# A transformer block in one kernel: the first layer norm's roots, the order of its loads and the order of the PSUM pools in the prologue

## The chip, the cores and the metric

The kernel runs on one core of one Trainium2 chip. The metric is the device time of one execution in microseconds (us); the time given for a kernel is the median of its runs.

The core has five engines, each with a queue of its own that is worked in order: TensorE (PE in the profile; its loads of stationary operands are shown apart, as PEld), VectorE (DVE), ScalarE (ACT), GpSimd (POOL) and SyncE (SP), which here issues nearly all transfers. Engines meet at semaphores. SBUF and PSUM are the two on-chip memories; matmuls write PSUM.

## The reference, cut to what matters

```python
S, D, H = 2048, 512, 32                      # batch 1, head size 16
def layernorm(x):                            # over the last axis, eps 1e-5
    return (x - mean(x)) / sqrt(var(x) + eps)

def attention(x, wqkv, wo):
    q, k, v = heads(x @ wqkv)
    p = softmax(einsum("bhqd,bhkd->bhqk", q, k) * Dh ** -0.5)
    return merge(einsum("bhqk,bhkd->bhqd", p, v)) @ wo

def gmlp(x, w_in, w_sp, b_sp, w_out):        # F = 1376, half of it 688
    z = gelu(x @ w_in)
    z1, z2 = z[..., :688], layernorm(z[..., 688:])
    return (z1 * (einsum("ts,bsf->btf", w_sp, z2) + b_sp)) @ w_out

h  = x + attention(layernorm(x), wqkv, wo)
h2 = h + gmlp(layernorm(h), w_in, w_sp, b_sp, w_out)
```

All arrays are float32, x is 2048 x 512.

## The kernel before

The 2048 rows are cut into 16 blocks of 128 rows (`sb`). Four stages follow each other: a prologue (layer norm of x and its projections), attention with the row maxima of the scores found ahead of their use, a stage per block of rows (h, the second layer norm, z), and the spatial product with the output. The first two stages are written inside `tc.manual_schedule` for TensorE, ScalarE, VectorE and SyncE: on these engines instructions stand in the order in which the program issues them; on GpSimd the framework orders them. Every change below lies in the prologue, but for the root `rstd_of`, which the second layer norm and that of z use too.

A product with more than half precision is made of three matmuls: operands are split into a high part (rounded, written by ScalarE or GpSimd) and a low part (the difference, by VectorE or GpSimd) in `split` (L77, L79 and L82 in the profile), and `mm3` (L85 to L87) multiplies high by high, high by low and low by high.

What happens to a block of x in the prologue:

- `load_x(sb)` (L261) asks for its 128 x 512 rows, 256 KB. All 10 buffers of tag `row` are shared with the pieces of the weights; `load_wv(d)` (L265) asks for a 128 x 512 piece of w_v and returns a function that splits it: the high part on ScalarE (for piece 1 on GpSimd), the low part on GpSimd.
- `stats` (L287, L288) finds mean and variance on VectorE; `scales` calls `rstd_of` for 1/sqrt(var + eps) and makes `nb` = -mean/sqrt (L301, L303).
- `rstd_of` (L92 to L109) takes a first guess from the bits of the number and improves it by three Newton steps. For one block (n = 1) a step is two instructions, each with operands that are one column; for more it is three.
- `normal` (L310) scales the block on ScalarE, in place.
- `turn_x` (L321) transposes it on TensorE into a PSUM tile `tp`; ScalarE copies the high part of the result into `xT[0]` and VectorE the low part into `xT[1]`.
- `proj_v` (L372 for blocks 0 and 1, else `mm3`) and `proj_qk` multiply; their accumulators come from `next_acc`, in turn two from pool `ps[0]` and one from `ps[1]`; `take` empties them (ScalarE and VectorE, L77 and L82, or VectorE alone, L382) and stores the result to DRAM.

Blocks 0 and 1 go through it one at a time, blocks 2 and 3 as a pair, blocks 4 to 15 in groups of four. `between` in `scales` lets the transposes of block 1 and the split of their result stand between the first and the second Newton step of blocks 2 and 3. While nothing is there to multiply, TensorE multiplies a tile of zeros, 16 times (L396).

In the later projections, the maxima of the first rows of scores are found between the products (`ahead`, `max_pair`, L203, L208). When the prologue's pools close, attention opens `ps_v` (one bank, the weighted sums `pv`, L628; the first time it is only written with a placeholder, L686) and `ps_s` (two tiles of two banks, the scores `s`, L617). They are allotted the banks that the prologue's pools had: pools are stacked in the order in which they are opened, and a tile waits for what its banks held before. Before the change that order is `pre_pt` (two banks), `pre_ps0` (two), `pre_ps1` (one). Each pair of key blocks in attention then goes: scores (L617), two maxima, `pv` of the pair before (L628), further maxima and scores, `pv`; ScalarE makes exponentials of the scores (L620).

Of the kernel before, what the change touches and what calls it, by code (L numbers as in the profile page):

```python
# [8 lines left out]
F32 = mybir.dt.float32  # L9
# [4 lines left out]
ALU = mybir.AluOpType  # L14
# [4 lines left out]
P = 128  # L19
S = 2048  # L20
D = 512
# [3 lines left out]
EPS = 1e-5  # L25
# [19 lines left out]
def block_kernel(ctx: ExitStack, tc: tile.TileContext, x, wqkv, wo, w_in, w_sp4, b_sp, w_out, out):  # L45
# [43 lines left out]
    def rstd_of(pool, var, n, between=lambda: None):  # L89

        hv = pool.tile([P, n], F32, name=f"rs_v{n}")
        nc.vector.tensor_scalar(hv, var, EPS, 0.5, op0=ALU.add, op1=ALU.mult)  # L92
        r = pool.tile([P, n], F32, name=f"rs_r{n}")
        nc.vector.tensor_scalar(r.bitcast(I32), hv.bitcast(I32), -0.5, GUESS,
                                op0=ALU.mult, op1=ALU.add)
        t = pool.tile([P, n], F32, name=f"rs_t{n}")
        for i in range(3):
            if i == 1:
                between()

            if n == 1:
                nc.vector.tensor_scalar(t, r, r, hv, op0=ALU.mult, op1=ALU.mult)
                u = pool.tile([P, 1], F32, name="rs_u", bufs=6)
                nc.vector.tensor_scalar(u, t, 1.5, r, op0=ALU.subtract, op1=ALU.mult)
                r = u
            else:
                nc.vector.tensor_mul(t, r, r)
                nc.vector.tensor_mul(t, t, hv)
                nc.vector.scalar_tensor_tensor(r, t, 1.5, r, op0=ALU.subtract, op1=ALU.mult)  # L109
        return r  # L110
# [135 lines left out]
    with ExitStack() as pre:  # L246
        p2 = pre.enter_context(tc.tile_pool(name="pre_2", bufs=2))
        pc = pre.enter_context(tc.tile_pool(name="pre_c", bufs=1))
        pt = pre.enter_context(tc.tile_pool(name="pre_pt", bufs=2, space=PSUM))
        ps = [pre.enter_context(tc.tile_pool(name=f"pre_ps{i}", bufs=2 - i, space=PSUM))  # L250
              for i in range(2)]
# [6 lines left out]

        def load_x(sb):
            xs[sb] = p2.tile([P, D], F32, name="xg", tag="row", bufs=10)  # L260
            nc.sync.dma_start(xs[sb], x[sb * P:(sb + 1) * P, :])  # L261

        def load_wv(d, eh="act"):
            t = p2.tile([P, 512], F32, name="wg", tag="row", bufs=10)
            nc.sync.dma_start(t, w4[:, d, 2 * D:])  # L265
            return lambda: split(wv[0][:, d, :], wv[1][:, d, :], t, eh, "pool")
# [16 lines left out]
        def stats(mv, *blocks):  # L283

            for sb in blocks:
                st = p2.tile([P, 6], F32, name="st")
                nc.vector.bn_stats(st, xs[sb])  # L287
# [6 lines left out]
        def scales(mv, between=lambda: None):  # L294
# [3 lines left out]
            rs = rstd_of(p2, t[:, :, 1], n, between)  # L298
            nb = p2.tile([P, n], F32, name=f"nb{n}")
            if n == 1:  # L300
                nc.vector.tensor_scalar(nb, rs, t[:, 0, 0:1], -1.0, op0=ALU.mult, op1=ALU.mult)  # L301
            else:
                nc.vector.scalar_tensor_tensor(nb, t[:, :, 0], -1.0, rs, op0=ALU.mult, op1=ALU.mult)  # L303
# [91 lines left out]
        for _ in range(16):  # L395
# [14 lines left out]
        with tc.manual_schedule(engines={E.PE, E.Activation, E.DVE, E.SP}):  # L410
# [14 lines left out]
            put = [load_wv(0), load_wv(1, "pool")]  # L425
            load_x(2)
            put.append(load_wv(2))
            load_x(3)
            put.append(load_wv(3))
            load_x(4)  # L430
            load_x(5)
            mv = [moments(1), moments(1), moments(2)]
            stats(mv[0], 0)
            normal = scales(mv[0])
            put[0]()
            put[1]()
            normal(0)
            stats(mv[1], 1)
            normal = scales(mv[1])
            put[2]()  # L440
            turn_x(0)
            load_x(6)
            put[3]()
            normal(1)
            stats(mv[2], 2, 3)
            chain = lambda d: d == 2 and normals.append(scales(mv[2], lambda: turn_x(1)))
            normals = []
            takes.append(proj_v(0, chain))
            normal = normals[0]
# [753 lines left out]
```

## Time and profile before

| what | us |
|---|---|
| median of 3 runs | 1889.48 |
| lowest and highest | 1888.72 and 1889.94 |
| the profiled execution | 1893.73 |
| its span, first to last instruction | 1891.8 |
| TensorE busy in the span | 1877.6 (99%) |
| VectorE, ScalarE, GpSimd busy | 1538.8, 1330.8, 209.3 |
| first steady matmul of the prologue (L85) | at 17.75 |
| first score of attention (L617) | at 173.28 |

A row of the timeline has the start, the length, engine and line, the operation, the tile written and those read, shapes and how many instructions are shown as one; in square brackets how long its engine had been idle and what ended that. Rows of a group have how many instructions, their busy time together and the mean of one in ns. Rows of a window have, for each engine, busy time and instructions, and at the end the granted clock of TensorE as a share, the share of the DMA engines and GB/s.

### The profile page before, as it was taken

The page shows a single profiled execution, that of the slowest core. Times are in us where ns is not written, and L with a number is a line of the kernel's source. Part 1 is how long each engine was busy: PE and PEld are TensorE (multiplying, and loading weights), DVE is VectorE, ACT ScalarE, POOL GpSimd, SP SyncE. Part 2 cuts the span into 40 slices and gives each one's busy share as a digit, 9 for nine tenths or more (in the row PEclk, how much of TensorE's full clock was granted, in tenths as well). Part 3 has the DMA queues.
Part 4 walks back from the last instruction along what each step waited for, and adds up shares of the span by engine and source line. Part 5 has one row for each costly group of instructions (what it writes and reads, how often), then busy time and mean ns, then how long its engine had stood idle before and what let it go on. Part 6 is the DMA issues. An engine that isn't in the chain of part 4 may idle for free.

```text
span 1891.8 us, 32405 instructions
## 1 busy us (share of the span) xinstructions
PE 1877.6 (99%) x11608; PEld 1065.0 (56%) x11608; DVE 1538.8 (81%) x3099; ACT 1330.8 (70%) x1733; POOL 209.3 (11%) x287
## 2 busy tenths in 40 slices
PE   9999999999999999999999999999999999999999
PEld 6865444444444444444444444444439999998887
DVE  6487999999999999999999999999926677867554
ACT  3334888888888888888888888888884444334221
POOL 2130000011010100000000000000010754001211
PEclk9999999999999999999999999999999999999999
DMA  6677111221120111021012011100024555677552
GB/s 188 186 192 192 43 24 27 49 53 28 38 56 22 47 38 25 19 51 32 14 44 36 23 30 38 24 16 14 10 78 138 163 167 170 215 216 238 177 185 75
DMA packets 148105, 159.82 MB, mean 84 GB/s; under 512 B 62952, under 2 KB 92664, under 8 KB 146408
## 3 DMA queue, kind: packets, MB, share of 16 engines
q1 hardware_dynamic: 143304, 146.48, 28.9%
q10 hardware_dynamic: 4608, 11.27, 1.6%
q8 instruction: 91, 1.49, 0.4%
q14 instruction: 70, 0.57, 0.1%
q0 software_dynamic: 32, 0.01, 0.0%
HBM read 101.16 MB, written 55.61 MB: 83 GB/s over the span
## 4 chain that ended last, share of the span: by engine, by line
PE 95%; DMA 2%; DVE 2%; issue 0%; POOL 0%; ACT 0%; SPq 0%; ACTq 0%; DVEq 0%; POOLq 0%
PE pv L628 27%; PE m L203 26%; PE s L617 13%; PE acc L85 6%; PE acc L87 6%; PE acc L86 6%; PE g L85 3%; PE g L86 3%; PE g L87 3%; DMA a<-in_w_sp 1%; PE tp L1093 0%; DMA g_scr<-q 0%; DMA h<-h_scr 0%; PE tp L804 0%; DMA rc<-r_scr 0%
## 5 line engine op out<-in xcount | busy, mean ns | idle before, releaser
L620 ACT ACTIVATE pt<-s 128x1024 f32<-128x1024 f32 x1024 | 993.2, 1030 | 147.4 <-PE s L617 145.0
L208 DVE TENSOR_REDUCE mx<-m 128x1 f32<-128x512 f32 x1511 | 959.0, 684 | 107.3 <-PE m L203 64.3
L203 PE MATMUL m<-kst,qst 48*128 48x512 f32 x1511 | 607.9, 448 | 0.0
L628 PE MATMUL pv<-pt,vst 128*32 128x512 f32 x4096 | 550.2, 605 | 0.7 <-ACT o L635 0.7
L617 PE MATMUL s<-qst,kst 50*128 50x512 f32 x2048 | 466.2, 428 | 2.0 <-DVE part L82 1.5
L203 PEld LDWEIGHTS m<-kst,qst 48*128 48x128 f32 x1511 | 263.8, 184 | 315.0 <-DVE mx L208 221.7
L617 PEld LDWEIGHTS s<-qst,kst 50*128 50x128 f32 x2048 | 223.6, 185 | 56.4 <-ACT pt L620 30.2
L203 PE MATMUL m<-uvs,qst 48*128 48x512 f32 x503 | 249.1, 496 | 0.0
L203 PEld LDWEIGHTS m<-uvs,qst 48*128 48x128 f32 x503 | 91.9, 183 | 208.1 <-DVE mx L208 205.3
L217 DVE CUSTOM_DVE_ANT_0 ab<-m,ab 128x512 f32<-128x512 f32 x252 | 171.8, 682 | 3.8 <-ACT ab L213 2.0
L628 PEld LDWEIGHTS pv<-pt,vst 128*32 128x32 f32 x4096 | 82.9, 108 | 161.0 <-issue 155.7
L213 ACT ACTIVATE ab<-m 128x512 f32<-128x512 f32 x251 | 151.0, 602 | 17.3 <-PE m L203 16.9
L79 POOL CAST mparts<-nm 128x16 fp32r<-128x16 f32 x32 | 6.3, 198 | 911.4 <-DVE nm L223 911.4
L747 ACT ACTIVATE ws<-a 128x512 fp32r<-128x512 f32 x80 | 45.8, 623 | 58.2 <-issue 37.4
L85 PE MATMUL acc<-wi,hT 128*128 128x344 f32 x256 | 83.1, 325 | 0.0
L87 PE MATMUL acc<-wi,hT 128*128 128x344 f32 x256 | 81.8, 319 | 0.0
L86 PE MATMUL acc<-wi,hT 128*128 128x344 f32 x256 | 81.7, 319 | 0.0
L819 ACT ACTIVATE z<-acc 128x344 f32<-128x344 f32 x64 | 29.2, 457 | 62.3 <-PE acc L87 54.8
L748 DVE TENSOR_TENSOR ws<-a,ws 128x512 fp32r<-128x512 f32 x80 | 56.5, 749 | 13.2 <-ACT ws L747 13.1
L85 PE MATMUL g<-b,ws 128*128 128x344 f32 x192 | 64.2, 334 | 0.0
L85 PE MATMUL g<-t,ws 128*128 128x344 f32 x192 | 61.3, 319 | 0.0
L86 PE MATMUL g<-b,ws 128*128 128x344 f32 x192 | 61.2, 319 | 0.0
(190 smaller groups left out, 2154.6 us busy)
## 6 DMA issues: line engine op xcount, KB each, us to landing
a<-in_w_sp SPq DMA_DIRECT2D x80, 256.0 KB
qst<-q_scr SPq DMA_DIRECT2D x192, 64.0 KB
kst<-k_scr SPq DMA_DIRECT2D x48, 256.0 KB
z_scr<-z ACTq DMA_DIRECT2D x32, 344.0 KB
k_scr<-part SPq DMA_DIRECT2D x16, 512.0 KB
q_scr<-part SPq DMA_DIRECT2D x16, 512.0 KB
z<-z_scr SPq DMA_DIRECT2D x14, 344.0 KB
b<-z_scr SPq DMA_DIRECT2D x24, 172.0 KB
```

Source lines behind the costliest of these rows:

```text
L85: nc.tensor.matmul(ps, lh, rh, start=first, stop=False)
L86: nc.tensor.matmul(ps, lh, rl, start=False, stop=False)
L87: nc.tensor.matmul(ps, ll, rh, start=False, stop=last)
L203: nc.tensor.matmul(acc, q[r, p, c], keys[r, p], start=True, stop=True)
L208: nc.vector.reduce_max(at(t, e if t else e - 1), acc, axis=AX.X)
L213: nc.scalar.activation(ab[0], acc, AF.Abs)
L217: nc.vector.tensor_tensor_reduce(ab[0], acc, ab[0], 0.5, LOW, ALU.add, ALU.max, at(0, 0))
L617: nc.tensor.matmul(s[:, t, :], k[r, p, kb * P:(kb + 1) * P], q[r, p, :], start=True, stop=True)
L620: nc.scalar.activation(t, s, AF.Exp, scale=DH ** -0.5)
L628: nc.tensor.matmul(pv[0][32 * j:32 * j + 32, :], vst[hg % 2][:, c:c + 32], pts[j % 2][:, j // 2, :], start=kb == 0, stop=kb == NB - 1)
L747: nc.scalar.activation(hi, src, AF.Copy)
L748: (nc.gpsimd if el == "pool" else nc.vector).tensor_sub(lo, src, hi.bitcast(F32))
```

## The change

- `rstd_of` makes one step of third order and one Newton step instead of three Newton steps: 9 instructions for more than one block (before 11), 7 for one (before 8). `between` is gone from it.
- Blocks 0 and 1 share one `scales` (n = 2), blocks 2 and 3 another.
- Block 0 is loaded, measured and scaled in two halves of 256 columns; the scaling of it moves from ScalarE to VectorE (new line 324, ahead of `nb`, line 327). TensorE's first two transposes wait for the first half, the other two for the second.
- The four pieces of w_v are asked for right behind blocks 0 and 1; blocks 2 to 5 follow. All four high parts are made on ScalarE, the first three ahead of anything else there, the low parts on GpSimd as before.
- The transposes of block 1 stand in `proj_v(0)` as before; the root of blocks 2 and 3 now follows the split of their result as a whole.
- The PSUM pools are opened in the order `pre_ps1`, `pre_ps0`, `pre_pt`.
- 15 matmuls of zeros instead of 16.

The order of the instructions that is built from it differs on TensorE by the one matmul of zeros alone; on ScalarE, GpSimd and SyncE in the first 20 instructions alone. Where waits moved: the first score waits for VectorE's reading of the accumulator before the last, and no longer of the last; the first `pv` waits for that of the last.

```diff
--- before.py
+++ after.py
@@ -86,28 +86,39 @@
         nc.tensor.matmul(ps, lh, rl, start=False, stop=False)
         nc.tensor.matmul(ps, ll, rh, start=False, stop=last)
 
-    def rstd_of(pool, var, n, between=lambda: None):
+    def rstd_of(pool, var, n):
+
+
+
+
 
         hv = pool.tile([P, n], F32, name=f"rs_v{n}")
-        nc.vector.tensor_scalar(hv, var, EPS, 0.5, op0=ALU.add, op1=ALU.mult)
-        r = pool.tile([P, n], F32, name=f"rs_r{n}")
+        nc.vector.tensor_scalar(hv, var, EPS, 32 / 729, op0=ALU.add, op1=ALU.mult)
+        r = pool.tile([P, n], F32, name=f"rs_r{n}", bufs=6)
         nc.vector.tensor_scalar(r.bitcast(I32), hv.bitcast(I32), -0.5, GUESS,
                                 op0=ALU.mult, op1=ALU.add)
         t = pool.tile([P, n], F32, name=f"rs_t{n}")
-        for i in range(3):
-            if i == 1:
-                between()
-
+
+        def squared():
             if n == 1:
                 nc.vector.tensor_scalar(t, r, r, hv, op0=ALU.mult, op1=ALU.mult)
-                u = pool.tile([P, 1], F32, name="rs_u", bufs=6)
-                nc.vector.tensor_scalar(u, t, 1.5, r, op0=ALU.subtract, op1=ALU.mult)
-                r = u
             else:
                 nc.vector.tensor_mul(t, r, r)
                 nc.vector.tensor_mul(t, t, hv)
-                nc.vector.scalar_tensor_tensor(r, t, 1.5, r, op0=ALU.subtract, op1=ALU.mult)
-        return r
+
+        def step(a, c, op, b):
+            out = pool.tile([P, n], F32, name=f"rs_r{n}", bufs=6)
+            if n == 1:
+                nc.vector.tensor_scalar(out, a, c, b, op0=op, op1=ALU.mult)
+            else:
+                nc.vector.scalar_tensor_tensor(out, a, c, b, op0=op, op1=ALU.mult)
+            return out
+
+        squared()
+        r = step(step(t, 5 / 3, ALU.subtract, t), 1.25, ALU.add, r)
+        squared()
+
+        return step(t, 2 / 3, ALU.subtract, r)
 
 
     attn = ctx.enter_context(ExitStack())
@@ -246,9 +257,9 @@
     with ExitStack() as pre:
         p2 = pre.enter_context(tc.tile_pool(name="pre_2", bufs=2))
         pc = pre.enter_context(tc.tile_pool(name="pre_c", bufs=1))
+        ps = {i: pre.enter_context(tc.tile_pool(name=f"pre_ps{i}", bufs=2 - i, space=PSUM))
+              for i in (1, 0)}
         pt = pre.enter_context(tc.tile_pool(name="pre_pt", bufs=2, space=PSUM))
-        ps = [pre.enter_context(tc.tile_pool(name=f"pre_ps{i}", bufs=2 - i, space=PSUM))
-              for i in range(2)]
         more[3] = more[4] = lambda: pt.tile([P, 512], F32, name="tp")
 
         xT = [pc.tile([P, DB, S], F32R, name=f"xT{i}") for i in range(2)]
@@ -256,14 +267,19 @@
         w4 = wqkv.rearrange("(a p) c -> p a c", p=P)
         xs, xns, wqk = {}, {}, {}
 
+        def columns(sb):
+
+            return [slice(c, c + D // 2) for c in (0, D // 2)] if not sb else [slice(0, D)]
+
         def load_x(sb):
             xs[sb] = p2.tile([P, D], F32, name="xg", tag="row", bufs=10)
-            nc.sync.dma_start(xs[sb], x[sb * P:(sb + 1) * P, :])
-
-        def load_wv(d, eh="act"):
+            for c in columns(sb):
+                nc.sync.dma_start(xs[sb][:, c], x[sb * P:(sb + 1) * P, c])
+
+        def load_wv(d):
             t = p2.tile([P, 512], F32, name="wg", tag="row", bufs=10)
             nc.sync.dma_start(t, w4[:, d, 2 * D:])
-            return lambda: split(wv[0][:, d, :], wv[1][:, d, :], t, eh, "pool")
+            return lambda: split(wv[0][:, d, :], wv[1][:, d, :], t, "act", "pool")
 
         def load_wqk(b):
             wqk[b] = [p2.tile([P, 2, DB, P], F32R, name=f"wqk{i}") for i in range(2)]
@@ -283,24 +299,32 @@
         def stats(mv, *blocks):
 
             for sb in blocks:
-                st = p2.tile([P, 6], F32, name="st")
-                nc.vector.bn_stats(st, xs[sb])
+                cs = columns(sb)
+                st = p2.tile([P, len(cs), 6], F32, name=f"st{len(cs)}")
+                for i, c in enumerate(cs):
+                    nc.vector.bn_stats(st[:, i, :], xs[sb][:, c])
                 nc.vector.bn_aggr(mv[0][:, len(mv) - 1, :], st)
                 mv.append(sb)
 
         def moments(n):
             return [p2.tile([P, n, 2], F32, name=f"mv{n}")]
 
-        def scales(mv, between=lambda: None):
+        def scales(mv, first=()):
+
+
+
 
             t, *blocks = mv
             n = len(blocks)
-            rs = rstd_of(p2, t[:, :, 1], n, between)
+            rs = rstd_of(p2, t[:, :, 1], n)
+            for sb in first:
+                j = blocks.index(sb)
+                xns[sb] = xs.pop(sb)
+                for c in columns(sb):
+                    nc.vector.tensor_scalar(xns[sb][:, c], xns[sb][:, c], t[:, j, 0:1],
+                                            rs[:, j:j + 1], op0=ALU.subtract, op1=ALU.mult)
             nb = p2.tile([P, n], F32, name=f"nb{n}")
-            if n == 1:
-                nc.vector.tensor_scalar(nb, rs, t[:, 0, 0:1], -1.0, op0=ALU.mult, op1=ALU.mult)
-            else:
-                nc.vector.scalar_tensor_tensor(nb, t[:, :, 0], -1.0, rs, op0=ALU.mult, op1=ALU.mult)
+            nc.vector.scalar_tensor_tensor(nb, t[:, :, 0], -1.0, rs, op0=ALU.mult, op1=ALU.mult)
 
             def normal(*which):
 
@@ -392,7 +416,7 @@
         idle = p2.tile([P, 512], BF, name="idle", bufs=1)
         nc.vector.memset(idle, 0.0)
         warm = ps[0].tile([P, 512], F32, name="acc")
-        for _ in range(16):
+        for _ in range(15):
             nc.tensor.matmul(warm, idle[:, :P], idle, start=True, stop=True)
 
         todo, done = [], [0]
@@ -422,31 +446,22 @@
 
             load_x(0)
             load_x(1)
-            put = [load_wv(0), load_wv(1, "pool")]
-            load_x(2)
-            put.append(load_wv(2))
-            load_x(3)
-            put.append(load_wv(3))
-            load_x(4)
-            load_x(5)
-            mv = [moments(1), moments(1), moments(2)]
-            stats(mv[0], 0)
-            normal = scales(mv[0])
-            put[0]()
-            put[1]()
-            normal(0)
-            stats(mv[1], 1)
-            normal = scales(mv[1])
-            put[2]()
+            put = [load_wv(d) for d in range(DB)]
+            for sb in range(2, 6):
+                load_x(sb)
+            mv = [moments(2), moments(2)]
+            stats(mv[0], 0, 1)
+            normal = scales(mv[0], (0,))
+            for d in range(3):
+                put[d]()
+            stats(mv[1], 2)
             turn_x(0)
-            load_x(6)
             put[3]()
             normal(1)
-            stats(mv[2], 2, 3)
-            chain = lambda d: d == 2 and normals.append(scales(mv[2], lambda: turn_x(1)))
-            normals = []
-            takes.append(proj_v(0, chain))
-            normal = normals[0]
+            stats(mv[1], 3)
+            load_x(6)
+            takes.append(proj_v(0, lambda d: d == 2 and turn_x(1)))
+            normal = scales(mv[1])
             load_x(7)
             put = load_wqk(0)
             proj(proj_v, 1)
```

## The prediction

> **What bounds the kernel now.** I read the chain of work that ended last first, then TensorE's waits, then the timeline of the first 18 us and of the step from the projections to attention.
>
> ```profile
> PE 95%; DMA 2%; DVE 2%; issue 0%; POOL 0%; ACT 0%; SPq 0%; ACTq 0%; DVEq 0%; POOLq 0%
> PE s L617 <- DVE part L82: 1.5, 1, 1.5
> PE acc L85 <- ACT xT L77: 0.8, 3, 0.3
> PE s L617 <- DVE mx L208: 0.6, 1, 0.6
> ```
>
> The chain is TensorE for 95%. The other rows are TensorE's waits from 20 to 1400 us (us in total, times, longest), first, second and last of four: 3.6 us in all, 1.5 of it in one piece. So what brings the first steady matmul (L85) forward, or closes that one gap, is kept to the end, and the start up to L85 is the only stretch where other engines set the pace.
>
> ```profile
> 0.74 2.69 DMA xg<-in_x
> 0.74 0.86 SPq L261 DMA_DIRECT2D xg<-in_x  x2
> 1.20 6.56 PE L396 MATMUL acc<-idle 128*128 128x512 bf16 x16 [1.20 <-DVE idle L393]
> 4.40 0.15 DVE L92 TENSOR_SCALAR rs_v<-mv 128x1 f32<-128x1 f32 x1
> 6.25 0.63 ACT L77 ACTIVATE wv<-wg 128x512 fp32r<-128x512 f32 x1 [4.23 <-DMA wg<-in_wqkv]
> 6.96 1.28 POOL L82 TENSOR_TENSOR wv<-wg,wv 128x512 fp32r<-128x512 f32 x1 [3.83 <-ACT wv L77]
> 7.73 0.63 PE L321 MATMUL tp<-ident,xg 128*128 128x128 f32 x4
> 8.24 0.63 ACT L77 ACTIVATE wv<-wg 128x512 fp32r<-128x512 f32 x1 [0.66 <-DMA wg<-in_wqkv]
> 8.78 0.58 ACT L77 ACTIVATE xT<-tp 128x512 fp32r<-128x512 f32 x1
> 8.95 3.80 POOL L82 TENSOR_TENSOR wv<-wg,wv 128x512 fp32r<-128x512 f32 x3 [0.16 <-ACT wv L77]
> 9.41 2.29 PE L372 MATMUL acc<-wv,xT 128*128 128x512 f32 x8 [1.05 <-ACT xT L77]
> 9.71 0.68 DVE L82 TENSOR_TENSOR xT<-tp,xT 128x512 fp32r<-128x512 f32 x1
> 11.54 0.60 PE L321 MATMUL tp<-ident,xg 128*128 128x128 f32 x4
> 12.04 0.84 DVE L92 TENSOR_SCALAR rs_v<-mv 128x2 f32<-128x2 f32 x1
> 14.18 0.15 DVE L107 TENSOR_TENSOR rs_t<-rs_r 128x2 f32<-128x2 f32 x1
> 15.34 0.16 DVE L303 SCALAR_TENSOR_TENSOR nb<-mv,rs_r 128x2 f32<-128x2 f32 x1
> 17.75 0.50 PE L85 MATMUL acc<-wv,xT 128*128 128x512 f32 x1
> ```
>
> Of the start: block 0 of x has landed at 3.43 (0.74 + 2.69), its transposes run at 7.73, its low half is split off on VectorE at 9.71, block 1's transposes run at 11.54, the scales of blocks 2 and 3 are ready at 15.50 (15.34 + 0.16), and L85 starts 2.25 us behind them.
>
> **The start, step by step.** *Loads.* The waits of ScalarE date w_v: first piece 6.25, third 8.24. Three transfers were asked for from the first to the third, so one lands each 0.66 us. x block 1, asked for right behind block 0, lands at about 3.43 + 0.66 = 4.1 (estimate); block 0 in halves adds an issue of 0.43 (half of 0.86), so 4.1 to 4.5; I take 4.25. The first w_v piece still has block 0 and 1 alone ahead of it: 6.25 to 6.7. Block 2, now behind all four, lands 2.65 later, 8.9 to 9.3.
>
> *VectorE.* Its statistics of block 0 wait for nobody. From landing to the first step of the root takes 0.97 (3.43 to 4.40), so 5.2. The joint root has nine steps (before: 8 for one block and again 8 for the next). Six such steps on two columns took 1.16 (14.18 to 15.34), 0.193 each: nine end at 6.94, and the first half of block 0 is asked for on VectorE at about 6.95.
>
> *Price of a half.* Before has no such form; the nearest rows:
>
> ```profile
> L717 DVE TENSOR_SCALAR hn<-xr,mv,rs_u 128x512 f32<-128x512 f32 x2 | 1.1, 547 | 0.1
> L102 DVE TENSOR_SCALAR rs_t<-rs_u,rs_v 128x1 f32<-128x1 f32 x68 | 18.6, 274 | 2.5
> 1576.76 0.94 POOL L844 TENSOR_TENSOR t<-z,z 128x344 f32<-128x344 f32 x1
> 1577.37 1.74 DVE L748 TENSOR_TENSOR ws<-s,ws 128x512 fp32r<-128x512 f32 x2
> 1577.63 0.94 POOL L745 CAST t<-z 128x344 fp32r<-128x344 f32 x1
> 1579.85 0.46 POOL L745 CAST t<-t 128x344 fp32r<-128x344 f32 x1
> ```
>
> 512 columns take 547 ns, one column 274 (both with two operands from SBUF), so 256 take about 0.41 us. But GpSimd stands in the way. The 0.84 us step at 12.04 is of the same operation; it normally takes 0.15 (4.40), and ended at 12.88, just behind GpSimd's last subtract (8.95 + 3.80 = 12.75): it was held until then. The rows at 1577 show the turns: VectorE's pair asked at 1577.37 waits for GpSimd's t (over at 1577.70), GpSimd's cast, 0.46 alone, is stretched to 0.94, over at 1578.57, and the pair ends at 1579.11, 0.54 behind it, so the cast went between the two. They alternate.
>
> The Trainium skill, SBUF — State Buffer, "Who interferes with whom", has a rule against this change: the pair of ports that VectorE and GpSimd share is an exclusive lock, which tensor_scalar may take, and a VectorE operation with two SBUF inputs meets GpSimd's reads at it. The 0.84 agrees; no run here shows it on 256 columns, and without the lock the start would be the first rival's.
>
> GpSimd's subtract starts 0.71 behind the landing of w_v (6.25 to 6.96): now at 6.96 to 7.4, I take 7.15, between VectorE's first half (6.95) and its second. So: first half 6.95 to 7.36; subtract 7.36 to 8.64; second half 8.64 to 9.05. Two transposes (half of 0.63) end at 9.45, ScalarE's high half (0.6) at 10.05, against 9.36 before. nb has two SBUF inputs and waits for the next subtract, to 10.33, and takes 0.16; statistics of block 2 (the 0.97 from above less a wait) end at 11.4; the low half of block 0 starts then, against 9.71. In before, 1.83 us lie from that start to block 1's transposes (9.71 to 11.54): now 13.2, ending at 13.8. High half 0.6, low half 0.6: 15.0. Before, half the root lay ahead of that low half; now all ten steps (nine and nb) follow, 1.93: 16.9. With the 2.25, L85 at 19.15: **1.4 us later**.
>
> Ends: if nothing blocks, block 2's landing at 8.9 to 9.3 sets the pace; its statistics end by 9.8 to 10.2 and the low half follows 1.2 to 1.6 ahead of the 11.4 above: L85 at 17.55 to 17.95. If w_v and block 2 land sooner by 0.7 or more as well, ScalarE sets it: second half done at 7.75, transposes 8.1, high half 8.8, last w_v piece 9.5, five products, block 1's transposes at 11.05 instead of 13.2: L85 at 17.0. If GpSimd is first both times, 20.45 (third rival).
>
> **The step to attention (PSUM order).**
>
> ```profile
> 171.42 0.40 PE L87 MATMUL acc<-xT,wqk 128*128 128x512 f32 x1
> 172.53 0.69 DVE L82 TENSOR_TENSOR part<-acc,part 128x512 fp32r<-128x512 f32 x1 [2.06 <-ACT part L77]
> 173.28 0.90 PE L617 MATMUL s<-qst,kst 50*128 50x512 f32 x4 [1.46 <-DVE part L82]
> 173.99 1.94 ACT L620 ACTIVATE pt<-s 128x1024 f32<-128x1024 f32 x2 [1.49 <-PE s L617]
> 174.34 1.91 PE L686 MATMUL pv<-vst 128*32 128x512 f32 x8
> 178.28 1.06 PE L628 MATMUL pv<-pt,vst 128*32 128x512 f32 x8
> 180.41 1.07 PE L628 MATMUL pv<-pt,vst 128*32 128x512 f32 x8
> 183.16 1.06 PE L628 MATMUL pv<-pt,vst 128*32 128x512 f32 x8
> 174.00:174.50 0.50, 0.50 (x8) 0.16 (x8) 0.05 (x1) 0.50 (x1) 0.00 (x0) 0.92 0.99 213
> 176.00:176.50 0.50, 0.50 (x6) 0.32 (x4) 0.00 (x0) 0.00 (x0) 0.00 (x0) 0.50 1.10 410
> 177.50:178.00 0.50, 0.50 (x5) 0.35 (x3) 0.37 (x2) 0.50 (x2) 0.00 (x0) 0.67 0.98 164
> ```
>
> The last projection ends at 171.82; the first scores wait 1.46 us until VectorE has emptied its bank (173.22). Then the granted clock (third number from the right of the windows) is half: 0.92 of a slice's 0.5 us puts its start at 174.42, 0.67 its end at 177.83, 3.41 us. In the changed program's waits, the first score waits only for the accumulator before the last, and the first pv for the last. So scores and two maxima go at 171.82 and need 1.06 (173.28 to 174.34); pv waits for 173.22 and starts at 173.27; nothing else of weight stands. At full clock the next pv of this place comes 2.75 later (180.41 to 183.16), at 176.02 instead of 178.28: **2.26 us sooner**; ScalarE's two exponentials (1.94 together, from 172.5 on) fit ahead of it. From there the beat is 4.88 (178.28 to 183.16). Low end: without the half clock in timed runs, before would come at 174.34 + 2.75 = 177.09, and 1.07 is gained. High end: the whole wait and half of the slow stretch, 1.46 + 1.71 = 3.17.
>
> The Trainium skill, TensorE: Matmul & The Clock Gate, "Why this matters for your kernels", puts the idle gap that loses the clock at about 3 us. The trace does not agree: 1.46 us was enough here, while the 1.05 us at 9.41 was not.
>
> **Costed at nothing.** Shorter roots elsewhere: of the five waits of TensorE from 1400 us on, none is on a root:
>
> ```profile
> PE tp L1093 <- ACT pr L1130: 2.3, 1, 2.3
> PE acc L87 <- DVE o L82: 0.3, 1, 0.3
> ```
>
> (first and last). One idle matmul less (0.41) is covered by the wait for the first transpose; without that cover it would gain at most its own 0.41. The same holds of moving VectorE's other steps: they are behind L85, under TensorE's steady work.
>
> **Sum.** +1.40 - 2.26 = -0.86 us. The profiled execution took 1893.73 (span 1891.8 and 1.9 around it), 4.25 above the median of 1889.48: it would become 1892.87, the median 1888.6. What a measurement can tell from no change is about 0.2%, 3.8 us.
>
> **The rivals.**
> 1. *The halves and the subtract do not meet* (w_v lands late enough, or this form is not held). For: w_v may be 0.45 later; against: GpSimd must start after 7.36. Start 0.05 sooner, sum -2.3: 1887.2. Chance 0.22.
> 2. *Faster by over 0.2%*: unblocked, w_v early (L85 at 17.0, 0.75 sooner), and the high end 3.17: -3.9, 1885.6. For: w_v no longer waits for block 2; against: the first piece has as much ahead of it as before. Chance 0.12.
> 3. *GpSimd first, twice*: it starts at 6.96 and VectorE later; the halves run at 8.24 and at 9.93, 1.3 behind the forecast: +2.7 - 2.26 = +0.4, 1889.9. Chance 0.12.
> 4. *Slower by over 0.2%: the start loses the clock.* As rival 3, but TensorE, through with the idle matmuls by 7.4, stands for over 1.46 us in one slow stretch, drops to half clock, and regains it only after a second: 2 x 1.71 on top, of which L85's steady work feels all. +2.7 + 3.4 - 2.26 = +3.84, and with the low end +5.0; 1894.0. It decides where the standing passes between 1.05 and 1.46. Chance 0.09.
> 5. *The new bank order frees nothing* (the scores wait for a load of q or k that VectorE's wait hid): +1.4, 1890.9. Chance 0.05.
> 6. *No half clock in timed runs of before*, as the page on the clock gate would have it: +1.40 - 1.07 = +0.3, 1889.8. Chance 0.08.
>
> **How the numbers follow.** The forecast has 0.32. Faster is rival 2, 0.12; slower rival 4, 0.09; the rest, 0.79, is within 0.2%. The range runs from rival 2's 1885.6 to 1893.0: it takes in all cases but most of rival 4 and half of rival 2.
>
> **What would show it.** Right: block 0's second half on VectorE at about 8.6 to 9.1 with a subtract between the halves; nb stretched over 1 us; L85 at 19.15; first scores right behind the last projection, no half clock there, pv's second at about 177.4 (176.02 + 1.4). Wrong: halves back to back and L85 before 18; a half clock within the first 25 us; or a wait of TensorE over 0.3 us ahead of the first scores.

## The result and the profile after

| kernel | median, us | to before, same chip (95% interval) |
|---|---|---|
| before | 1889.61 | |
| after | 1895.93 | 1.0033 [1.0022, 1.0045] |

The changed kernel is 6.3 us slower (medians of six runs each; the three of before shown above are among them). The profiled execution of it took 1896.7, its span 1894.9.

The start, in the timeline of after. The rows answer to those of before up to its L85 at 17.75.

```profile
1.20 5.82 PE L420 MATMUL acc<-idle 128*128 128x512 bf16 x15 [1.20 <-DVE idle L417]
5.75 0.69 DVE L305 BATCH_NORM_STATS2 st<-xg 128x6 f32<-128x512 f32 x1 [1.74 <-DMA xg<-in_x]
6.42 0.63 ACT L77 ACTIVATE wv<-wg 128x512 fp32r<-128x512 f32 x1 [4.39 <-DMA wg<-in_wqkv]
7.10 0.16 DVE L106 TENSOR_TENSOR rs_t<-rs_r 128x2 f32<-128x2 f32 x1
7.13 3.71 POOL L82 TENSOR_TENSOR wv<-wg,wv 128x512 fp32r<-128x512 f32 x3 [3.99 <-ACT wv L77]
7.29 1.12 DVE L107 TENSOR_TENSOR rs_t<-rs_t,rs_v 128x2 f32<-128x2 f32 x1
8.45 1.19 DVE L114 SCALAR_TENSOR_TENSOR rs_r<-rs_t 128x2 f32<-128x2 f32 x1
9.67 1.18 DVE L114 SCALAR_TENSOR_TENSOR rs_r<-rs_r,rs_r 128x2 f32<-128x2 f32 x1
10.89 0.16 DVE L106 TENSOR_TENSOR rs_t<-rs_r 128x2 f32<-128x2 f32 x1
11.47 0.74 DVE L324 TENSOR_SCALAR xg<-xg,mv,rs_r 128x256 f32<-128x256 f32 x2
12.03 1.09 PE L345 MATMUL tp<-ident,xg 128*128 128x128 f32 x4 [5.02 <-DVE xg L324]
13.81 3.78 PE L396 MATMUL acc<-wv,xT 128*128 128x512 f32 x8 [0.69 <-ACT xT L77]
18.09 4.66 PE L396 MATMUL acc<-wv,xT 128*128 128x512 f32 x16
23.89 0.50 PE L85 MATMUL acc<-wv,xT 128*128 128x512 f32 x1
```

Three things follow each other. Block 1's statistics (5.75) wait 1.74 for its landing, so the joint root begins late. Its third step starts at 7.10, GpSimd's first subtract at 7.13, and the three two-column steps that follow take 1.12, 1.19 and 1.18 instead of 0.16: one for each of the three subtracts (3.71 together). From its first step at 6.69 to its last at 11.44 the root takes 4.75. Once they are over, the next step takes 0.16 again. And TensorE, through with its zeros at 7.02, stands for 5.02.

The granted clock (third number from the right) shows what the standing costs, in the windows of after:

```profile
8.00:9.00 1.00, 0.00 (x0) 0.00 (x0) 0.96 (x2) 0.49 (x1) 1.00 (x2) 1.00 1.03 385
9.00:10.00 1.00, 0.00 (x0) 0.00 (x0) 0.97 (x2) 0.00 (x0) 1.00 (x2) 0.76 1.05 404
12.00:13.00 1.00, 0.97 (x4) 0.72 (x4) 0.96 (x4) 0.00 (x0) 0.00 (x0) 0.50 0.00 0
19.00:20.00 1.00, 1.00 (x4) 0.77 (x3) 0.86 (x3) 0.07 (x1) 0.00 (x0) 0.62 0.00 0
```

0.76 and 0.62 of these windows put the half clock at 9.52 to 19.76, and the first eight products take 3.78 where before's took 2.29. L85 comes 6.14 behind before's.

The step to attention, in the timeline of after, and TensorE's wait there:

```profile
178.92 0.39 PE L87 MATMUL acc<-xT,wqk 128*128 128x512 f32 x1
179.24 0.74 PE L632 MATMUL s<-qst,kst 50*128 50x512 f32 x4
180.78 1.07 PE L701 MATMUL pv<-vst 128*32 128x512 f32 x8 [0.55 <-DVE part L82]
183.52 1.07 PE L643 MATMUL pv<-pt,vst 128*32 128x512 f32 x8
```

```profile
PE tp L1108 <- ACT pr L1145: 0.6, 1, 0.6
PE pv L701 <- DVE part L82: 0.6, 1, 0.6
```

The scores go right behind the last projection, the wait has moved to pv, and pv's second comes 4.21 after the projections end (179.31), just as forecast (176.02 less 171.82); in the profile of before it was 6.46. So the forecast gain is there, between these two profiles.

Between these two places lies a loss that nothing in the prediction names. L85 came 6.14 late; the last projection, 7.49. Nearly all of it builds up evenly in the products with w_q and w_k. First before, then after (ns of one: least, median, most; then first and last start):

```profile
L85 PE MATMUL acc<-xT,wqk x128: 388/392/509, 23.6 to 171.0; 128*128 128x512 f32 x128
L87 PE MATMUL acc<-xT,wqk x128: 388/388/398, 24.1 to 171.4; 128*128 128x512 f32 x128
```

```profile
L85 PE MATMUL acc<-xT,wqk x128: 393/398/502, 29.8 to 178.5; 128*128 128x512 f32 x128
L87 PE MATMUL acc<-xT,wqk x128: 390/397/405, 30.2 to 178.9; 128*128 128x512 f32 x128
```

Same count, same shape, but 148.7 us from first to last where before needed 147.4; they stand 233 ns apart instead of 229. The products with w_v kept their pace, 228 on the mean in both.

### The profile page after: what moved, and what is told of

It reads as the page before. It is cut to its first block, busy times and chain, and to the rows that moved or that the text cites. A ratio compares the mean times of both kernels' runs of the same rounds, so it can differ in the third digit from the quotient of the medians.

```text
span 1894.9 us, 32357 instructions
## 1 busy us (share of the span) xinstructions
PE 1879.4 (99%) x11607; PEld 1066.2 (56%) x11607; DVE 1528.0 (81%) x3054; ACT 1330.5 (70%) x1733; POOL 208.6 (11%) x286
## 4 chain that ended last, share of the span: by engine, by line
PE 98%; DVE 1%; DMA 0%; ACT 0%; issue 0%; SPq 0%; ACTq 0%; DVEq 0%
PE pv L643 27%; PE m L214 26%; PE s L632 13%; PE acc L85 7%; PE acc L87 6%; PE acc L86 6%; PE g L85 4%; PE g L87 4%; PE g L86 4%; PE tp L1108 1%; PE tp L819 0%; PE tp L345 0%; DMA xg<-in_x 0%; PE tp L214 0%; PE acc L396 0%
## 5 line engine op out<-in xcount | busy, mean ns | idle before, releaser
L85 PE MATMUL acc<-wi,hT 128*128 128x344 f32 x256 | 83.1, 325 | 0.0
L85 PE MATMUL g<-b,ws 128*128 128x344 f32 x192 | 64.2, 334 | 0.0
L85 PE MATMUL g<-t,ws 128*128 128x344 f32 x192 | 61.3, 319 | 0.0
L86 PE MATMUL g<-t,ws 128*128 128x344 f32 x192 | 61.2, 319 | 0.0
```

The lines of the kernel that those rows point to most:

```text
L85: nc.tensor.matmul(ps, lh, rh, start=first, stop=False)
L86: nc.tensor.matmul(ps, lh, rl, start=False, stop=False)
```

## The experiments

All twelve, with L85 (the first of `mm3` in the prologue) as the profile of each has it, and the spacing of the products with w_q and w_k. Ratios are to before on the same chip; those whose intervals overlap are not told apart by time alone. L85 is of one profile each, and landings move it: e1 has before's start, yet its first piece of w_v was there at 5.58 instead of 6.25, and its L85 is 0.67 sooner. The interval of after, [1.0022, 1.0045], overlaps with those of e2, e3, e4, e5 and e7; what these show rests on their rows first.

| kernel | L85 at | ns apart | median | ratio (95% interval) |
|---|---|---|---|---|
| e1_psum_only | 17.08 | 229 | 1888.50 | 0.9989 [0.9981, 0.9998] |
| e2_whole_load | 21.77 | 233 | 1893.83 | 1.0018 [1.0009, 1.0027] |
| e3_idle38 | 20.97 | 233 | 1894.80 | 1.0024 [1.0014, 1.0033] |
| e4_own_roots | 20.01 | 233 | 1894.83 | 1.0023 [1.0013, 1.0033] |
| e5_gate | 20.31 | 233 | 1893.49 | 1.0017 [1.0008, 1.0026] |
| e6_mended | 18.39 | 229 | 1890.59 | 1.0001 [0.9992, 1.0010] |
| e7_places | 22.22 | 229 | 1893.04 | 1.0015 [1.0007, 1.0024] |
| e8_root_psum | 17.62 | 229 | 1888.01 | 0.9987 [0.9978, 0.9996] |
| e9_wv_sooner | 17.00 | 229 | 1887.44 | 0.9987 [0.9979, 0.9996] |
| e10_halves | 17.74 | 229 | 1889.05 | 0.9995 [0.9986, 1.0004] |
| e11_both | 17.71 | 229 | 1889.17 | 0.9996 [0.9986, 1.0005] |
| e12_idle15 | 18.96 | 229 | 1891.28 | 1.0005 [0.9996, 1.0014] |

**The bank order alone.** Before, with

```diff
+        ps = {i: pre.enter_context(tc.tile_pool(name=f"pre_ps{i}", bufs=2 - i, space=PSUM))
+              for i in (1, 0)}
         pt = pre.enter_context(tc.tile_pool(name="pre_pt", bufs=2, space=PSUM))
-        ps = [...]
```

> The kernel before with the three PSUM pools opened in the changed order and nothing else. Theory (the loss lies in the start, and the new bank order is a gain): L85 stays at 17.75, the first scores follow the last projection within 0.3 us, no half clock behind them, 1.1 to 2.3 us faster than before (1887.3 to 1888.5). Rival (the new order itself slows the projections, whose matmuls stand 233 ns apart after the change against 229 before): the step from L85 to the last projection is 1.2 us longer than before, and the time is that of before within 1 us.

0.9989: a gain, 1.4 us from the 1889.88 of before beside it; the interval holds 1.07 us as well as 2.26. The scores go right behind the last projection (171.04, its end 171.11) and no half clock follows. The products keep 229 ns, so the bank order is not what slows them.

**Block 0 by one transfer**, in after (`load_x` without the loop over `columns`):

```diff
-            for c in columns(sb):
-                nc.sync.dma_start(xs[sb][:, c], x[sb * P:(sb + 1) * P, c])
+            nc.sync.dma_start(xs[sb], x[sb * P:(sb + 1) * P, :])
```

> The changed kernel with block 0 loaded by one transfer again; its statistics and scaling stay in halves. Theory (the extra transfer makes block 1 the third one asked for, and the third lands late; the joint root then runs into GpSimd's subtracts): statistics of block 1 start at about 4.1 to 4.5 instead of 5.75, no step of the joint root is longer than 0.3 us, L85 at 19 to 20.6 instead of 23.9, 3 to 5 us faster than the changed kernel (1891 to 1893). Rival (block 1 is late for another reason, or the half clock alone makes the loss): L85 and the time stay as after the change, 1895.9, or the root is short and L85 stays above 22.

Block 1 is there when its statistics start at 4.33, near the prediction's 4.25, and the root starts at 5.22. It is held all the same, in its last two steps, so "no step over 0.3 us" did not come true, nor did the ranges: L85 at 21.77, the time 1893.83. Timeline:

```profile
6.42 0.16 DVE L106 TENSOR_TENSOR rs_t<-rs_r 128x2 f32<-128x2 f32 x1
6.48 3.71 POOL L82 TENSOR_TENSOR wv<-wg,wv 128x512 fp32r<-128x512 f32 x3 [3.35 <-ACT wv L77]
6.61 1.15 DVE L107 TENSOR_TENSOR rs_t<-rs_t,rs_v 128x2 f32<-128x2 f32 x1
7.80 1.19 DVE L114 SCALAR_TENSOR_TENSOR rs_r<-rs_t,rs_r 128x2 f32<-128x2 f32 x1
9.02 1.64 DVE L323 TENSOR_SCALAR xg<-xg,mv,rs_r 128x256 f32<-128x256 f32 x2
```

Here w_v landed sooner too, and the subtract starts at 6.48. Between a root that ends at 6.9 at best (5.20 and 1.74, as in e6) and a subtract that starts anywhere from 6.10 (e7) to 7.13 (after) there is little or no room: the late landing made it worse, but the root is held without it too.

**The clock kept up**, in after:

```diff
-        for _ in range(15):
+        for _ in range(38):
```

> The changed kernel with 38 matmuls of zeros instead of 15, so that TensorE has work until block 0 is scaled. Theory (part of the loss is the half clock from 9.5 to 19.8): clock full from about 6 us on, the eight products at 13.8 take 1.9 instead of 3.8 us, L85 at 21.3 to 22.1, 1.8 to 2.6 us faster than the changed kernel (1893.3 to 1894.1). Rival A (the half clock is the whole loss): L85 below 19, 1890 or less. Rival B (it costs nothing, since VectorE sets the pace): 1895.9.

The clock stays full, and the three root steps are held as before. The same products in its timeline:

```profile
12.96 2.12 PE L396 MATMUL acc<-wv,xT 128*128 128x512 f32 x8 [0.69 <-ACT xT L77]
15.27 3.94 PE L396 MATMUL acc<-wv,xT 128*128 128x512 f32 x16
```

2.12 against 3.78 and 3.94 against 4.66: the half clock is worth 2.4 us of after's start. (L85 came 2.9 sooner; block 1 was also there 0.66 sooner than in after.) The median fell by 1.1 us only and lies above the expected range; see what stays open.

**Separate roots**, in after:

```diff
-            mv = [moments(2), moments(2)]
-            stats(mv[0], 0, 1)
-            normal = scales(mv[0], (0,))
+            mv = [moments(1), moments(2), moments(1)]
+            stats(mv[0], 0)
+            scales(mv[0], (0,))
+            stats(mv[2], 1)
+            normal = scales(mv[2])
```

> The changed kernel with a root of its own for block 0 and another for block 1 (same polynomial, one column, seven steps), block 0 scaled ahead of block 1's statistics. Theory (the joint root waits for block 1 and three of its two-input steps wait for GpSimd): block 0 scaled by about 6.5, no step of the roots over 0.3 us, L85 at 18.2 to 20.2, 4 to 5.5 us faster than the changed kernel (1890.4 to 1892). Rival (the roots cost the same either way and w_v's place sets L85): less than 1.5 us faster.

```profile
5.94 0.74 DVE L324 TENSOR_SCALAR xg<-xg,mv,rs_r 128x256 f32<-128x256 f32 x2
6.79 4.95 POOL L82 TENSOR_TENSOR wv<-wg,wv 128x512 fp32r<-128x512 f32 x4 [3.65 <-ACT wv L77]
8.67 1.19 PE L396 MATMUL acc<-wv,xT 128*128 128x512 f32 x4 [1.10 <-ACT xT L77]
8.78 0.27 DVE L104 TENSOR_SCALAR rs_t<-rs_r,rs_v 128x1 f32<-128x1 f32 x1
9.34 1.20 DVE L327 SCALAR_TENSOR_TENSOR nb<-mv,rs_r 128x1 f32<-128x1 f32 x1
11.27 0.66 DVE L82 TENSOR_TENSOR xT<-tp,xT 128x512 fp32r<-128x512 f32 x1
11.99 1.20 PE L396 MATMUL acc<-wv,xT 128*128 128x512 f32 x4 [2.12 <-DVE xT L82]
```

The first product comes at 8.67, sooner than in before. Block 1's one-column root runs beside GpSimd's subtracts unheld (0.27 for a squaring, as ever); its `nb`, which has two tiles from SBUF as inputs, is held (1.20). But block 0's low half then stands behind all that on VectorE, TensorE waits 2.12 for it and loses the clock. Of the 4 to 5.5 us expected for the time, 1.1 are there, which is in the rival's range, though its reason is not what the rows show.

**The subtracts behind the root**, in after:

```diff
+        gate = pc.tile([P, 2], F32, name="gate")
...
+            if first:
+                nc.gpsimd.tensor_copy(gate, rs)
```

> Kernel after, and ahead of the three low parts of w_v GpSimd copies the joint root's two columns into a tile of its own. So GpSimd's subtracts, which in the profile after run from 7.13 to about 10.8, cannot start before the root has ended. Theory (the subtracts hold VectorE's two-input steps; three of them took 1.12, 1.19 and 1.18 us instead of 0.16): all nine steps of the root take 0.06 to 0.16 us, the root ends 3 us sooner (about 8.5 instead of 11.45), TensorE's first product comes 2 to 3 us sooner, line 85's first product of block 0 with the low rows at 21 to 22.5 instead of 23.89, and the time is 1.5 to 3 us under the kernel after (1893 to 1894.4). Rival (the root is late because of the landing alone, or GpSimd's later subtracts are missed by the products): no gain, 1895.5 to 1897.

```profile
7.45 0.16 DVE L114 SCALAR_TENSOR_TENSOR rs_r<-rs_t,rs_r 128x2 f32<-128x2 f32 x1
7.65 1.69 DVE L325 TENSOR_SCALAR xg<-xg,mv,rs_r 128x256 f32<-128x256 f32 x2
7.82 5.12 POOL L82 TENSOR_TENSOR wv<-wg,wv 128x512 fp32r<-128x512 f32 x4
9.26 1.22 DVE L330 SCALAR_TENSOR_TENSOR nb<-mv,rs_r 128x2 f32<-128x2 f32 x1
20.31 0.50 PE L85 MATMUL acc<-wv,xT 128*128 128x512 f32 x1
```

The same nine steps now take 1.74 (5.87 to 7.61) instead of 4.75: the subtracts hold the root, shown. The median falls by 2.4 us, within the range. L85 is sooner than expected, as block 1 was also there 0.83 sooner than in after; that part is luck. With the root out of the way, the two halves and `nb` do just what the prediction said: first half, subtract, second half (1.69 for both instead of 0.74), `nb` 1.22.

**The tiles at before's places**, in after:

```diff
-        r = pool.tile([P, n], F32, name=f"rs_r{n}", bufs=6)
+        r = pool.tile([P, n], F32, name=f"rs_r{n}", bufs=8 if n == 1 else 2)
...
-            out = pool.tile([P, n], F32, name=f"rs_r{n}", bufs=6)
+            out = b
             if n == 1:
+                out = pool.tile([P, n], F32, name=f"rs_r{n}", bufs=8)
...
-            nb = p2.tile([P, n], F32, name=f"nb{n}")
+            nb = p2.tile([P, n + 48 * (n == 2)], F32, name=f"nb{n}")[:, :n]
```

> Kernel after with the same instructions in the same order, but the small tiles of the root are reused in place and the last of them padded, so that x transposed, w_v, w_q and w_k and all later large tiles lie at the same places in SBUF as in the kernel before (in the kernel after they lie 128 to 256 bytes per partition lower). Theory (the place sets the pace): the products of x transposed with w_q and w_k stand 229 ns apart as before, instead of 233.3, those of the output projection 229 instead of 231, and the time is 1.2 to 2 us under the kernel after (1893.9 to 1894.7). Rival (the pace comes from the changed order of loads or steps): 233 ns, 1895.5 to 1896.5.

```profile
L85 PE MATMUL acc<-xT,wqk x128: 388/392/509, 28.1 to 175.4; 128*128 128x512 f32 x128
L87 PE MATMUL acc<-xT,wqk x128: 388/388/398, 28.5 to 175.9; 128*128 128x512 f32 x128
```

The durations of before to the nanosecond, and 147.3 from first to last. The instructions are after's; only the places of the small tiles, and with them of all large ones, differ. So the places set the pace, shown; which of the moved tiles does it is not. The median, 1893.04, is below the expected range, and not all of its 2.9 us under after is the places' doing: the slower products with w_q and w_k were 1.3, while in this profile block 1 was also there 1.04 sooner and the half clock shorter (9.10 to 15.93).

**All four mended at once**: e2, e5, e7 and 23 idle products.

> Kernel after with four things mended at once: block 0 by one transfer, GpSimd's subtracts behind the root as in e5_gate, 23 idle products instead of 15, and the tiles back at the places in SBUF that they had before (as in e7_places). Theory (the start, 6.1 us, and the slower pace of the products with w_q and w_k, 1.2 us, are the whole loss and the transition's gain of 2.2 is there): line 85's first product at 17.5 to 19, no half clock, products 229 ns apart, time 1886.8 to 1889. Rival (the joint root and its late start keep 2 us or more, or the loss lies behind the start): 1890 to 1893.

L85 at 18.39, 229 ns, a full clock in the profile, and 1.0001: what was named accounts for the loss, but for the 1.7 us or so that the interval leaves on either side. The median is 1.6 above the expected range and lies in the rival's (before, beside it, took 1890.44), and five of the eleven runs list a clock of 0.999: mended, the change stands level with before and gains nothing on it that can be measured.

**Part by part on top of before.** e8 is e1 with the new root (at before's places; two blocks' root and separate ones as before); e9 adds the order of the loads, e10 the halves of block 0, e11 both:

```diff
 e9:
-            put = [load_wv(0), load_wv(1, "pool")]
-            load_x(2)
-            put.append(load_wv(2))
...
+            put = [load_wv(0), load_wv(1, "pool"), load_wv(2), load_wv(3)]
+            for sb in range(2, 6):
+                load_x(sb)
 e10 (the loads and statistics in halves are as in the change):
...
+            if blocks == [0]:
+                xns[0] = xs.pop(0)
+                for c in columns(0):
+                    nc.vector.tensor_scalar(xns[0][:, c], xns[0][:, c], t[:, 0, 0:1], rs,
+                                            op0=ALU.subtract, op1=ALU.mult)
+                return
```

> Kernel before with two parts of the change alone: the PSUM pools opened in the changed order (as e1_psum_only, which took 1888.5) and every root of one or more columns by the step of third order and one of Newton's, 7 steps for one block instead of 8, at the same places in SBUF. The blocks' order, loads and first rows stay as before. Theory (the root's steps alone are worth 0.1 to 0.4 us at the start and hardly anything later): 1888.0 to 1888.5, ratio to before 0.9985 to 0.999. Rival (the shorter root brings GpSimd's subtracts or the transposes into its way): 1889.5 or more.

> Kernel e8_root_psum (before, with the changed order of the PSUM pools and the third-order root, large tiles at before's places) with one more part of the change: all four parts of w_v are asked for ahead of blocks 2 to 5, where e8 has block 2 between the second and third part and block 3 between the third and fourth. Theory (the parts of w_v are not what the start waits for; in the profile of e8 ScalarE waits 0.68 and 0.24 us for them, and blocks 2 and 3 land later for it): line 85's first product within 0.5 us of e8's 17.62 and the time within 0.7 us of e8's ratio 0.9987. Rival (blocks 2 and 3, whose sums stand ahead of the next root, become the wait): line 85 over 1 us later, ratio over 0.9992.

> Kernel e8_root_psum with one more part of the change: block 0's row is fetched in two halves, its sums are taken in halves and VectorE normalizes the halves right behind block 0's own root, instead of ScalarE behind the first part of w_v. The other loads, block 1 and the roots stay as in e8. Theory (halves alone help, it was the joint root that cost): block 0's transposes at 6.3 to 7.0 instead of 7.58, first product at 8.0 to 8.8 instead of 9.28, line 85's first product 0.3 to 1 us before e8's 17.62, time 0.2 to 1 us under e8's ratio (0.9982 to 0.9986). Rival (the third transfer asked for lands late, it is now block 1, and TensorE waits for block 1 what it gained on block 0): line 85 no sooner than 17.6, ratio 0.9987 to 0.9995.

> Kernel e8_root_psum with both e9's order of loads and e10's halves, so that all parts of the changed kernel are in it but the joint root of blocks 0 and 1, the loads' places in SBUF and the later merging of blocks 2 and 3 behind it. Theory: the sum of e9 and e10, line 85's first product at 16.6 to 17.6, ratio 0.998 to 0.9988. Rival (the order of loads and the late landing of block 1 add up): line 85 at 18 or later, half clock in the start, ratio 0.9993 or more.

e8 and e9 keep e1's gain and show no loss; e9 has the lowest median here, 1887.44, and is faster than before and after, but time does not tell it from e1 and e8. Its L85 is 0.62 ahead of e8's, but its first piece of w_v happened to be there 0.45 sooner (ScalarE starts on it at 5.65, not 6.10); e1, in the old order and with that piece at 5.58, has 17.08, so little of the 0.62 is the order. e10 and e11 show no gain on e8, against their theories. e10's ratio is the one its rival gave, but not for the rival's reason: block 1's statistics did not wait for its landing. The timeline of e10:

```profile
2.45 5.17 PE L418 MATMUL acc<-idle 128*128 128x512 bf16 x13
5.78 1.84 DVE L318 TENSOR_SCALAR xg<-xg,mv,rs_r 128x256 f32<-128x256 f32 x2
6.19 1.28 POOL L82 TENSOR_TENSOR wv<-wg,wv 128x512 fp32r<-128x512 f32 x1 [3.05 <-ACT wv L77]
7.45 0.67 PE L343 MATMUL tp<-ident,xg 128*128 128x128 f32 x4
8.20 0.63 ACT L77 ACTIVATE wv<-wg 128x512 fp32r<-128x512 f32 x1 [2.10 <-DMA wg<-in_wqkv]
8.73 0.58 ACT L77 ACTIVATE xT<-tp 128x512 fp32r<-128x512 f32 x1
```

GpSimd's subtract starts at 6.19, so the first half is done by then; but TensorE works through its zeros until 7.45 first, and a subtract comes between the halves. In e11 the halves met no subtract (0.73 for both, from 5.70), and the transposes stood at 7.45 all the same. A second thing stands behind them in both: the transposes end at 8.1, but ScalarE has a piece of w_v ahead of the high half of block 0 and gets it at 8.20 (8.18 in e11), so the high half starts at 8.73 (8.72), where e8 has 8.65.

e11 stands level with before, so the loss lies in what it leaves out. That is more than its expectation names: besides the joint root, the places and the merging of blocks 2 and 3, it keeps 16 products of zeros and w_v as before splits it, with one subtract and the high part of piece 1 on GpSimd (6.39 and 7.61) where after has three subtracts in a row. No run has the joint root beside that old split.

**One idle product less**, before with `range(15)`, and with it a second profile of the old step to attention:

> Kernel before with 15 idle products instead of 16, the smallest part of the change alone, and with it a second look at the step to attention in the old order of the PSUM pools. Theory (the half clock after the 1.46 us wait of the first scores, seen in the one profile of before, is not what its runs usually have: of 89 runs of before beside these experiments 58 list a mean clock of 1.000, and the 3.41 us at half clock alone would make it 0.999): mean clock 1.000 in most runs, the scores still wait about 1.46 us for VectorE, and where the profiled run has 1.000 the second product of pv comes 3.8 us behind the first scores instead of 5.0; the time is within 0.7 us of before. Rival (the half clock there is the rule): mean clock 0.999 in most runs and 5.0 us in the profile. Second rival (the idle product missing lets the clock fall in the start): time over 1.5 us above before, mean clock 0.998 or less in most runs.

```profile
172.63 0.40 PE L87 MATMUL acc<-xT,wqk 128*128 128x512 f32 x1
174.49 0.91 PE L617 MATMUL s<-qst,kst 50*128 50x512 f32 x4 [1.46 <-DVE part L82]
178.29 1.07 PE L628 MATMUL pv<-pt,vst 128*32 128x512 f32 x8
```

```profile
175.00:176.00 1.00, 1.00 (x9) 0.35 (x10) 0.33 (x1) 0.80 (x1) 0.00 (x0) 1.00 1.09 221
177.00:178.00 1.00, 1.00 (x9) 0.62 (x5) 0.87 (x2) 1.00 (x3) 0.00 (x0) 1.00 1.06 356
```

The same wait of 1.46, and the clock stays full: pv's second comes 3.80 behind the scores, where the profile of before had 5.00. Of 104 runs of before in the four sets, 71 list a mean clock of 1.000; the 3.41 us at half clock would make it 0.999. So most runs of before do not have that stretch. The idle product itself: 1.0005, an interval on both sides of 1; 6 of e12's 11 runs list a clock below 1.000, 2 of the 15 of before beside them, so it may well cost some. Its profile did lose the clock in the start, from 10.68 to 14.09: the zeros were through at 5.89, TensorE stood 1.84 ahead of the transposes and 1.53 ahead of the first product, and L85 came at 18.96. But those 15 products took 4.70, in other profiles 5.21 to 5.94, so one product less is not all of it. It isn't settled.

## Why the prediction was wrong

By its own steps:

- *Block 1 lands at 4.25.* Its statistics began at 5.75 in after, at 4.71, 4.92 and 5.09 in e7, e5 and e3, and at 4.33 with block 0 whole (e2, where they waited for nothing). The step took the pace of later pieces (0.66) and half an issue; a third transfer came 0.5 to 1.5 later than that.
- *The joint root ends at 6.94, and the first half comes ahead of the subtract at 7.15.* This is the step that failed: the root ended at 11.44, 4.5 late, 1.5 of it by block 1's landing and 3.0 by the hold. The mechanism was right and put on the wrong instructions: the 0.84 us row of before that showed a two-column step held by GpSimd was applied to `nb` and the halves, which come after the root, but not to the root's own steps, because the estimate left them 0.21 us of room. Their price, 0.193 each, came from rows at 14.18 to 15.34, when GpSimd had been through with its subtracts since 12.75. Three held steps cost 3.0 (the root took 4.75 instead of 1.74), and e5 took them away. The halves then found GpSimd idle, and the hold that was forecast for them, which e5, e2 and e10 show as described, was never met in after.
- *Rival 4, the start loses the clock.* It happened, but by the root, not by GpSimd coming first at the halves. It was priced as two stretches of 3.41 us, 3.4 in all; after's profile has three in a row (10.24), and e3 puts what the products lost by it at 2.4, so the nearness of the two figures is luck. Its bound, a standing between 1.05 and 1.46, does not hold (see the last section).
- *The step to attention, 2.26 sooner.* Against the profiled execution, right to 0.01. But that execution was one with a half clock that most runs lack: against e12, pv's second comes 4.21 instead of 5.26 behind the projections, 1.05. That is the low end of 1.07, the term of rival 6, which had a chance of 0.08.
- *Costed at nothing.* With the root's new tiles (no one-column ones in the prologue, six buffers for the others) all later large tiles came to lie 128 to 256 bytes per partition lower, as e7's expectation has it, and the products with w_q and w_k slowed by 2%. The prediction counted instructions and has no step for this.
- *The sum.* In place of +1.40 - 2.26 stands +6.14 (L85) + 1.3 (148.7 less 147.4) - 1.05 = +6.4; the medians differ by 6.3. That they meet so closely is partly luck: L85 is of one profile on each side, and after's lists a mean clock of 0.997, four of its six runs 0.998.

What stays open: why the third transfer lands late; why a product's pace depends on where the tiles lie (no layout was tried for its own sake but before's); what decides when the clock falls; and why e3 and e4 are 1.5 and 2.4 us slower against before than such a sum makes them. In their profiles TensorE's single wait for ScalarE's `pr` in the last stage is 1.6 and 1.7, against 0.6 in after, 2.3 in before and 0.8 in e12, so one profile can differ from another by 2 us there.

## What to carry to other kernels

When a change joins small steps or moves them, list each instruction of the moved chain against what GpSimd is doing at that time: a two-column step of 0.16 us becomes 1.2 us beside a 128x512 subtract, while the one-column form with column operands runs freely, so the shorter chain can be the slower one. A margin of 0.2 us between two things that start by DMA landings, which differ by up to 1 us from profile to profile, is no margin; and a gain read from one profiled execution that lies 4 us above the median should first be asked whether the median has it at all. After any change of tile counts, compare the spacing of the steady matmuls.

## What was not expected of the hardware

- *The places of tiles.* With the large SBUF tiles 128 to 256 bytes per partition lower, 128x512 products stood 233 ns apart instead of 229, and 229 again when they were moved back (e7, e6). Those of the output projection went from 229 to 231 and back alike; those with w_v did not change.
- *Which small steps are held beside GpSimd's subtract.* Held: two-column steps with two tiles from SBUF (1.12 to 1.23), one-column `nb` in the form with two tiles (1.20), and the two-column first step with one input (0.84 in before, 0.61 in e9, 1.14 to 1.15 in e8, e11 and e12, each over 0.11 to 0.13 behind the end of a subtract). Not held: one-column steps whose other operands are columns (0.15 to 0.28), statistics of 512 columns (0.68). The Trainium skill, SBUF — State Buffer, "Who interferes with whom", names two SBUF inputs and tensor_scalar as what meets GpSimd at the shared ports; these rows agree, and the one-column rows show a form that doesn't.
- *When the clock falls.* In after, e7 and e2 it fell 2.5, 2.3 and 2.1 us into one long standing of TensorE. In e4, in the start of e12 and in the profile of before it fell when TensorE was at work again, 1.2, 0.8 and 1.1 us behind waits of 2.12, 1.53 and 1.46; a wait of 1.46 kept it in e12's step to attention. So no length of a single wait decides it here, and what does is not shown. What the windows do show is how long it stays away: 3.41 us in before, e4 (13.17 to 16.58), e5 (11.71 to 15.12) and e12, 6.83 in e2 (8.80 to 15.63) and e7, 10.24 in after, once, twice or three times the same length. In 1890 us one such stretch makes a mean clock of 0.999, two make 0.998, three 0.997, so the clock that a run lists hints at how many it had. The Trainium skill, TensorE: Matmul & The Clock Gate, "Why this matters for your kernels", warns of gaps over about 3 us; the standings of after, e7 and e2 (5.02, 4.20 and 3.78) agree with that, the losses behind 1.46, 1.53 and 2.12 do not.
